# Attention in fp32 with clustered masks, then two mixing layers, on one core: TensorE's order pinned by unit

## The chip, the cores and the metric

The kernel runs on one core of a Trainium2 chip. The metric is the device time of one execution in microseconds (us); the median of three runs before the change is 664.98 us (664.54 to 666.16).

## What is computed

`reference` runs three stages on fp32 data, with 2 batches, 8 heads, 768 positions and a head size of 64 (so a model width of 512):

```python
mask = q_assign[:, :, :, None] == k_assign[:, :, None, :]        # 16 clusters per head
scores = np.where(mask, scale * q @ k.T, -1e9)
attn = np.exp(scores - scores.max(-1)) ; attn /= attn.sum(-1) + 1e-9
x = (attn @ v)                       # put back to (2, 768, 512)
u = x + token_mlp(x) ; x = u + relu(u @ w_ch1) @ w_ch2
x = x + w_tok_r @ (x cos(x @ w_theta)) + w_tok_i @ (x sin(x @ w_theta))
out = x + relu(x @ w_ch)
```

The change lies in the first of these stages, the attention.

## The kernel before, in words

The attention takes up roughly the first 240 us of the span. It is cut into 48 **units**: for each of 16 (batch, head) pairs, three blocks of 256 query positions. One unit passes through three functions:

- `scores` (L380): two score tiles, one per 128 queries. A tile is 4 products of 128x384 (L397 and L398: the high part of q with k, then the low part of q together with the mask's rows). It lands in a PSUM buffer of the pool `ps_s`, which has **two** buffers, so a tile needs the buffer of the tile two before it. VectorE (DVE) takes the maximum (L400, `nm`), ScalarE (ACT) the exponential (L402, `e`), and after the exponential the buffer is free.
- `turn` (L409): 12 transposes of 128x128 on TensorE (PE) of the unit's two `e` tiles, four to each of three PSUM tiles `t` (L417). The pool `ps_t` has **three** buffers. ACT copies the first two out, DVE the third (L420, L422, `p`).
- `values` (L426): the product of `p` with v. The program issues six matrix products, the profile shows twelve records of 128x256 in column halves of 64 (L438, `o`), into the **one** buffer of the pool `ps_o`. ACT copies one half out (L445, `tmp`), DVE adds the other to it (L447, `xt`).

The loop over `n` (L485) calls `scores` of unit n, `turn` of unit n-1 and `values` of unit n-2. Other work of the loop also uses `ps_t`: once in six units the masks of the next pair of heads (L246 `sim`, one tile; L270 `pp`, one tile, read by DVE at L271 `oh`), and once in six units `natural` (L451), which transposes a finished pair of heads (L460 `x`, two tiles of 4 and 2 transposes) and multiplies each block by its reciprocal sum on DVE (L462 `xn`, six instructions). The `x` tiles come up eight times in all: at six places with a `pp` beside them, a seventh near the end of the loop and the last behind it. Near the end, the weights of the next stage are also prepared inside the loop (L109 to L116 on ACT, DVE and POOL).

The order in which an engine's instructions stand is set by a scheduler when the program is built (`schedule_with_timeline_sim=True`, L799 of the launch); each engine then runs its own list from top to bottom. `tc.issue_after(i)` forces the instructions of its block that are on i's engine behind i; it adds no wait between engines. Before the change, only `values` was tied in this way (the call at L532 and L533, behind the last transpose that the text had issued). Scores and transposes were free to be placed by the scheduler.

Of the kernel before, what the change touches and what calls it, by code (L numbers as in the profile page):

```python
# [49 lines left out]
def tile_model(ctx: ExitStack, tc: tile.TileContext, qT, kT, v, cent, w1, w2, wc1, wc2, wth, wri, wch, out):  # L50


    nc = tc.nc
# [14 lines left out]
    marks = {}  # L68
# [92 lines left out]
    with ExitStack() as actx:  # L161
# [12 lines left out]
        def warm_up(n):  # L174
            for _ in range(n):
                nc.tensor.matmul(wps[:, :256], warm[:, :P], warm, start=True, stop=True)
# [203 lines left out]
        def scores(b, h, u, ops):  # L380

            qh, ql, k1, kk, _ = ops
            es = []
            for j in range(2):
                qt = 2 * u + j
                c = slice(qt * P, qt * P + P)
                ps = ps_s.tile([P, 2, 512], F32, tag="s", name=f"s{b}{h}{qt}")
                first = (b, h, u) == (0, 0, 0)
                if first:

                    for half in range(2):
                        nc.tensor.matmul(ps[:, half, :NH], qh[:, c], k1[:, half * NH : half * NH + NH], start=True, stop=False)
                with tc.issue_after(marks["cl"].ins) if first else nullcontext():
                    for half in range(2):
                        n = slice(half * NH, half * NH + NH)
                        if not first:
                            nc.tensor.matmul(ps[:, half, :NH], qh[:, c], k1[:, n], start=True, stop=False)  # L397
                        marks["scores"] = nc.tensor.matmul(ps[:, half, :NH], ql[:, c], kk[:, n], start=False, stop=True)  # L398
                nm = small.tile([P, 1], F32, tag="nm", bufs=4, name=f"nm{b}{h}{qt}")
                marks["max"] = nc.vector.tensor_reduce(out=nm, in_=ps[:, :, :NH], axis=AX.XY, op=ALU.max, negate=True)  # L400
                e = ap.tile([P, S], F32, tag="e", bufs=4, name=f"e{b}{h}{qt}")
                marks["exp"] = nc.scalar.activation(  # L402
                    out=e.rearrange("p (a n) -> p a n", a=2), in_=ps[:, :, :NH], func=AF.Exp,
                    bias=nm, accum_out=sums[b, h // 2][:, qt, h % 2 : h % 2 + 1],
                )
                es.append(e)
            return es

        def turn(b, h, u, es):  # L409

            pr = []
            for j in range(NT // 2):
                ps = ps_t.tile([P, 2, 256], F32, tag="t", name=f"t{b}{h}{u}{j}")
                for i in range(2):
                    for a in range(2):
                        kt = 2 * j + a
                        marks["turn"] = nc.tensor.transpose(ps[:, a, i * P : i * P + P], es[i][:, kt * P : kt * P + P], ident)  # L417
                p = ap.tile([P, 2, 256], F32, tag="p", bufs=PB, name=f"p{b}{h}{u}{j}")
                if KINDS[j] == "A":
                    marks["pA"] = nc.scalar.activation(out=p, in_=ps, func=AF.Copy)  # L420
                else:
                    marks["pV"] = nc.vector.tensor_copy(out=p, in_=ps)  # L422
                pr.append(p)
            return pr

        def values(us):  # L426


            if us[-1][0] == len(units) - 1:
                ps = ps_s.tile([P, 2, 512], F32, tag="s", name="olast")[:, 0, :]  # L430
            else:
                ps = ps_o.tile([P, 512], F32, tag="o", name=f"o{us[0][0]}")
            outs = []
            for i, (n, pr, vs) in enumerate(us):
                po = ps[:, 256 * i : 256 * i + 256]
                for kt in range(NT):
                    r = 64 * (kt % 2)
                    nc.tensor.matmul(  # L438
                        po[r : r + 64, :], vs[:, kt, :], pr[kt // 2][:, kt % 2, :], start=kt < 2, stop=kt >= NT - 2,
                        tile_position=(0, r),  # L440
                    )
                outs.append((units[n], po))
            for (b, h, u), po in outs:
                tmp = ap.tile([64, 256], F32, tag="tmp", bufs=2, name=f"tmp{b}{h}{u}")
                marks["tmp"] = nc.scalar.activation(out=tmp, in_=po[64:128, :], func=AF.Copy)  # L445
                r0 = 64 * (h % 2)
                nc.vector.tensor_tensor(  # L447
                    out=xts[b, h // 2][r0 : r0 + 64, u * 256 : u * 256 + 256], in0=po[0:64, :], in1=tmp, op=ALU.add
                )
# [25 lines left out]
        with tc.issue_after(marks["cst"].ins):  # L475
            ops = {heads[0]: prep_pair_first(raws) + (vs00,)}
# [5 lines left out]
        units = [(b, h, u) for b, h in heads for u in range(NT // 2)]  # L482
        es, prs = {}, {}
        late, group = [], []
        for n in range(len(units) + SKEW):  # L485
            if n < len(units):
                b, h, u = units[n]
                if u == 0 and h % 2 == 0:
                    sums[b, h // 2] = small.tile([P, NT, 2], F32, tag="sm", bufs=2, name=f"sm{b}{h}")
                    xts[b, h // 2] = ap.tile([P, S], F32, tag="xt", bufs=2, name=f"xt{b}{h}")  # L490
                if n != 1:
                    es[n] = scores(b, h, u, ops[b, h])
                if n == 0:
                    next(first, None)
                    place(1, ms[0, 0])
                    scored = marks["scores"]
                    es[1] = scores(*units[1], ops[b, h])
                    with tc.issue_after(marks["max"].ins):
                        ops[heads[1]] = prep_first(*heads[1])
                    marks["scores"] = scored  # L500
                    for w, k in zip(WARM[1:], ("cps", "sim", "scores")):
                        with tc.issue_after(marks[k].ins):
                            warm_up(w)
                h1 = n // 3 + 1
                if 1 < h1 < len(heads) and u == PREP[h1 % 2]:
                    b2, h2 = heads[h1]
                    ops[b2, h2] = prep(b2, h2, ms[b2, h2 // 2])
                p1 = n // 6 + 1
                if p1 < len(heads) // 2:
                    pr = heads[2 * p1][0], heads[2 * p1][1] // 2  # L510
                    if n % 6 == PAIR_AT[0]:
                        raws = load_pair(*pr)
                    if n % 6 == PAIR_AT[1]:
                        split_pair(*pr, raws)
                    if n % 6 == PAIR_AT[2]:
                        gen = masks(*pr)
            if n >= 3:
                for _ in range(PACE):
                    next(gen, None)
            if n == 42:  # L520
                mctx.close()
            if 0 <= n - 1 < len(units):
                prs[n - 1] = turn(*units[n - 1], es.pop(n - 1))
            if n < 3:
                with tc.issue_after((marks["turn"] if n else marks["scores"]).ins):
                    for _ in range(PACE):
                        next(gen, None)
            if 0 <= n - SKEW:
                b, h, u = units[n - SKEW]
                group.append((n - SKEW, prs.pop(n - SKEW), ops[b, h][4]))  # L530
                if len(group) == GROUP:
                    with tc.issue_after(marks["turn"].ins):  # L532
                        values(group)  # L533
                    group = []
                if h % 2 == 1 and u == NT // 2 - 1:
                    late.append((n + 1, b, h // 2))
            while late and (n >= late[0][0] or n == len(units) + SKEW - 1):
                _, b, pr = late.pop(0)
                natural(b, pr)
            if n in X_AT:  # L540
                tok_x(0, X_AT.index(n), part, "pp")
            if n in W1_AT:
                with tc.issue_after(marks["exp"].ins):
                    i = len(w1s)
                    w1s.append(load_w(w1[:, i * 512 : i * 512 + 512], f"w1_{i}", W1_AT[n]))
            if n == len(units):
                with tc.issue_after(marks["tmp"].ins), tc.issue_after(marks["pA"].ins), tc.issue_after(marks["pV"].ins):
                    for i in range(NT // 2):
                        w2s.append(load_w(w2[:, :, i * 256 : i * 256 + 256], f"w2_{i}", "pv"))
# [197 lines left out]
    for n in range(len(steps) + 2):  # L747
        if n < len(steps):
            t, b = steps[n]
# [53 lines left out]
```

## Time and profile before

| What | Value |
|---|---|
| median of 3 runs | 664.98 us |
| the profiled execution | 664.99 us, its span 663.3 us |
| PE busy | 646.8 us (98%), 3591 matmuls |
| DVE / ACT / POOL busy | 401.2 / 344.9 / 257.6 us |
| costliest groups of the attention on PE | L417 80.5 us, L397 71.9 us, L438 71.2 us, L398 65.3 us (they overlap) |

The page's busy share of PE counts matmuls that overlap in the array's pipeline, so 98% does not say that nothing can be won. The chain of waits is of more use: it lists, in order of time, the work that led to the last instruction, with the time by which each piece moved the end forward. Where a piece of the chain is not PE's, PE stood and waited for it. One unit's pieces there add up to the unit's time.

### The profile page before, as it was taken

The page shows a single profiled execution, that of the slowest core. Times are in us where ns is not written, and L with a number is a line of the kernel's source. Part 1 is how long each engine was busy: PE and PEld are TensorE (multiplying, and loading weights), DVE is VectorE, ACT ScalarE, POOL GpSimd, SP SyncE. Part 2 cuts the span into 40 slices and gives each one's busy share as a digit, 9 for nine tenths or more (in the row PEclk, how much of TensorE's full clock was granted, in tenths as well). Part 3 has the DMA queues.
Part 4 walks back from the last instruction along what each step waited for, and adds up shares of the span by engine and source line. Part 5 has one row for each costly group of instructions (what it writes and reads, how often), then busy time and mean ns, then how long its engine had stood idle before and what let it go on. Part 6 is the DMA issues. An engine that isn't in the chain of part 4 may idle for free.

```text
span 663.3 us, 9795 instructions
## 1 busy us (share of the span) xinstructions
PE 646.8 (98%) x3591; PEld 517.7 (78%) x3591; DVE 401.2 (60%) x649; ACT 344.9 (52%) x653; POOL 257.6 (39%) x231
## 2 busy tenths in 40 slices
PE   7999999999999989999999999999999999999998
PEld 4777777777777758878888888888887878888886
DVE  5877778687787776466665442546677694531212
ACT  5676776777767863256444320428487673320000
POOL 6230312364031131138887520603467796541000
PEclk9999999999999998999999999999999999999999
DMA  8554755444555121023433310310021424300001
GB/s 294 160 138 105 169 123 144 120 117 114 113 123 124 37 96 47 18 67 124 154 133 127 126 53 14 95 33 0 1 85 42 128 88 127 114 20 33 16 33 47
DMA packets 24207, 61.42 MB, mean 93 GB/s; under 512 B 4256, under 2 KB 7520, under 8 KB 24160
## 3 DMA queue, kind: packets, MB, share of 16 engines
q1 hardware_dynamic: 24160, 60.80, 32.3%
q8 instruction: 28, 0.46, 0.3%
q14 instruction: 19, 0.16, 0.1%
HBM read 39.65 MB, written 3.15 MB: 65 GB/s over the span
## 4 chain that ended last, share of the span: by engine, by line
PE 86%; ACT 4%; DVE 3%; POOL 3%; issue 2%; DMA 2%; SPq 0%; POOLq 0%; ACTq 0%
PE o L438 10%; PE t L417 9%; PE s L397 5%; PE r L126 5%; PE r L127 5%; PE r L128 5%; PE c L126 5%; PE c L127 5%; PE c L128 5%; PE s L398 5%; PE y L128 4%; PE y L127 4%; PE y L126 4%; PE po L126 2%; PE po L128 2%
## 5 line engine op out<-in xcount | busy, mean ns | idle before, releaser
L402 ACT ACTIVATE e<-s,nm 128x768 f32<-128x768 f32 x96 | 86.7, 905 | 29.4 <-DVE nm L400 28.1
L400 DVE TENSOR_REDUCE nm<-s 128x1 f32<-128x768 f32 x96 | 90.5, 951 | 18.9 <-PE s L398 18.0
L417 PE MATMUL t<-ident,e 128*128 128x128 f32 x576 | 80.5, 275 | 0.6 <-ACT p L420 0.5
L417 PEld LDWEIGHTS t<-ident,e 128*128 128x128 f32 x576 | 66.4, 140 | 16.0 <-issue 9.4
L397 PE MATMUL s<-k,qh 128*128 128x384 f32 x188 | 71.9, 382 | 2.5 <-ACT e L402 2.3
L438 PE MATMUL o<-p,vs 128*64 128x256 f32 x564 | 71.2, 388 | 0.0
L398 PE MATMUL s<-k,q 128*128 128x384 f32 x192 | 65.3, 343 | 2.4 <-DVE q L279 2.4
L420 ACT ACTIVATE p<-t 128x512 f32<-128x512 f32 x96 | 52.2, 594 | 25.4 <-PE t L417 25.0
L126 PE MATMUL r<-ul,c_h 128*128 128x512 f32 x144 | 56.5, 396 | 0.4 <-DVE ul L90 0.4
L126 PE MATMUL y<-zl,k_h 128*128 128x512 f32 x144 | 56.1, 390 | 0.0
L128 PE MATMUL y<-zh,k_h 128*128 128x512 f32 x144 | 56.1, 390 | 0.0
L127 PE MATMUL r<-uh,c_l 128*128 128x512 f32 x144 | 56.1, 390 | 0.0
L127 PE MATMUL y<-zh,k_l 128*128 128x512 f32 x144 | 56.0, 389 | 0.0
L127 PE MATMUL c<-c_h,rl 128*128 128x512 f32 x144 | 56.0, 390 | 0.0
L128 PE MATMUL r<-uh,c_h 128*128 128x512 f32 x144 | 56.0, 390 | 0.0
L128 PE MATMUL c<-c_h,rh 128*128 128x512 f32 x144 | 55.9, 390 | 0.0
L126 PE MATMUL c<-c_l,rh 128*128 128x512 f32 x144 | 55.2, 391 | 0.0
L438 PEld LDWEIGHTS o<-p,vs 128*64 128x64 f32 x564 | 36.3, 136 | 22.7 <-issue 5.9
L116 POOL TENSOR_TENSOR c_f<-c_f,c_raw 128x512 uint32<-128x512 uint32 x24 | 31.6, 1318 | 44.7 <-issue 31.3
L80 POOL TENSOR_SCALAR qh<-ql 128x768 fp32r<-128x768 f32 x7 | 5.8, 835 | 100.9 <-DMA qh<-qh 100.8
L397 PEld LDWEIGHTS s<-k,qh 128*128 128x128 f32 x188 | 35.4, 188 | 11.1 <-ACT e L402 5.6
L398 PEld LDWEIGHTS s<-k,q 128*128 128x128 f32 x192 | 36.7, 192 | 3.8 <-ACT k L276 3.4
(192 smaller groups left out, 1387.9 us busy)
## 6 DMA issues: line engine op xcount, KB each, us to landing
c_raw<-wc SPq DMA_DIRECT2D x24, 512.0 KB, 3.3
k_raw<-wri SPq DMA_DIRECT2D x18, 512.0 KB, 3.5
qh<-qh SPq DMA_DIRECT2D x28, 192.0 KB, 3.0
k<-kh SPq DMA_DIRECT2D x28, 192.0 KB, 3.8
ql<-qT SPq DMA_DIRECT2D x8, 384.0 KB, 3.2
kl<-kT SPq DMA_DIRECT2D x8, 384.0 KB, 4.6
vs<-v SPq DMA_DIRECT2D x16, 192.0 KB, 2.4
w_raw<-w SPq DMA_DIRECT2D x6, 512.0 KB, 4.1
```

Of the source, the lines that this page charges most:

```text
L80: nc.gpsimd.tensor_scalar(out=h, in0=x, scalar1=1.0, scalar2=0.0, op0=ALU.mult, op1=ALU.add)
L116: nc.gpsimd.tensor_tensor(out=wu, in0=wu, in1=lo, op=ALU.add)
L126: nc.tensor.matmul(ps, ah, bl, start=first and i == 0, stop=False)
L127: nc.tensor.matmul(ps, al, bh, start=False, stop=False)
L128: nc.tensor.matmul(ps, ah, bh, start=False, stop=last and i == n - 1)
L397: nc.tensor.matmul(ps[:, half, :NH], qh[:, c], k1[:, n], start=True, stop=False)
L398: marks["scores"] = nc.tensor.matmul(ps[:, half, :NH], ql[:, c], kk[:, n], start=False, stop=True)
L400: marks["max"] = nc.vector.tensor_reduce(out=nm, in_=ps[:, :, :NH], axis=AX.XY, op=ALU.max, negate=True)
L402: marks["exp"] = nc.scalar.activation(out=e.rearrange("p (a n) -> p a n", a=2), in_=ps[:, :, :NH], func=AF.Exp, bias=nm, accum_out=sums[b, ...
L417: marks["turn"] = nc.tensor.transpose(ps[:, a, i * P : i * P + P], es[i][:, kt * P : kt * P + P], ident)
L420: marks["pA"] = nc.scalar.activation(out=p, in_=ps, func=AF.Copy)
L438: nc.tensor.matmul(po[r : r + 64, :], vs[:, kt, :], pr[kt // 2][:, kt % 2, :], start=kt < 2, stop=kt >= NT - 2, tile_position=(0, r),)
```

## The change

Two ties are added. `scores` of unit n goes behind the last product of `values` that the text has issued (unit n-3), and `turn` of unit n-1 goes behind the last score product that the text has issued (unit n). With the tie that was there, the list on PE becomes: scores of n, transposes of n-1, values of n-2, scores of n+1, and so on. No arithmetic, buffer or transfer is changed. `marks` is a dictionary of the last instruction of each kind.

```diff
-                    nc.tensor.matmul(
+                    marks["o"] = nc.tensor.matmul(
                         po[r : r + 64, :], vs[:, kt, :], pr[kt // 2][:, kt % 2, :], start=kt < 2, stop=kt >= NT - 2,
                         tile_position=(0, r),
                     )
...
                 if n != 1:
-                    es[n] = scores(b, h, u, ops[b, h])
+                    with tc.issue_after(marks["o"].ins) if "o" in marks else nullcontext():
+                        es[n] = scores(b, h, u, ops[b, h])
...
             if 0 <= n - 1 < len(units):
-                prs[n - 1] = turn(*units[n - 1], es.pop(n - 1))
+                with tc.issue_after(marks["scores"].ins) if n > 2 else nullcontext():
+                    prs[n - 1] = turn(*units[n - 1], es.pop(n - 1))
```

In the built program PE's list changes in the attention alone. DVE's and ACT's lists change there too, since the scheduler places their work anew around it. The lists of POOL and of SP, which issues the DMAs, stay as they were.

A plain unit on PE (in the names `s_435` is a score tile, `t_467` a tile of transposes, `e_387` and `e_396` the two exponentials that it is made from):

```order
 L398 MATMUL s_435<-k_1_152,q_1_150 128x384
-L417 MATMUL t_467<-ident,e_387 128x128 x2
-L417 MATMUL t_474<-ident,e_387 128x128 x2
-L417 MATMUL t_481<-ident,e_387 128x128 x2
 L397 MATMUL s_444<-k_243,qh_242 128x384
 L398 MATMUL s_444<-k_1_152,q_1_150 128x384
 L397 MATMUL s_444<-k_243,qh_242 128x384
 L398 MATMUL s_444<-k_1_152,q_1_150 128x384
+L417 MATMUL t_467<-ident,e_387 128x128 x2
 L417 MATMUL t_467<-ident,e_396 128x128 x2
+L417 MATMUL t_474<-ident,e_387 128x128 x2
 L417 MATMUL t_474<-ident,e_396 128x128 x2
```

The transposes of the first exponential stood between the two score tiles; now both score tiles come first and the twelve transposes follow in one piece.

The same engine at a place where `natural` stands. Ahead of these rows both programs have one score tile (`s_1126`), the six `x` transposes and `pp`:

```order
 L397 MATMUL s_1135<-k_941,qh_940 128x384
 L398 MATMUL s_1135<-k_1_152,q_1_150 128x384
-L397 MATMUL s_1181<-k_941,qh_940 128x384
-L398 MATMUL s_1181<-k_1_152,q_1_150 128x384
-L397 MATMUL s_1181<-k_941,qh_940 128x384
-L398 MATMUL s_1181<-k_1_152,q_1_150 128x384
 L417 MATMUL t_1150<-ident,e_1063 128x128 x2
 L417 MATMUL t_1150<-ident,e_1072 128x128 x2
```

The first score tile of the next unit (`s_1181`) stood between this unit's scores and the transposes. Now the transposes follow at once, and that tile comes behind the values.

DVE at the same place, in the changed program:

```order
L400 TENSOR_REDUCE nm_1131<-s_1126 128x1
L447 TENSOR_TENSOR xt_921<-o_1099,tmp_1106 64x256
L462 TENSOR_TENSOR xn_66<-x_1112,ri_1109 128x128
L462 TENSOR_TENSOR xn_67<-x_1112,ri_1109 128x128
L462 TENSOR_TENSOR xn_68<-x_1112,ri_1109 128x128
L462 TENSOR_TENSOR xn_69<-x_1112,ri_1109 128x128
L462 TENSOR_TENSOR xn_70<-x_1121,ri_1109 128x128
L462 TENSOR_TENSOR xn_71<-x_1121,ri_1109 128x128
L271 SCALAR_TENSOR_TENSOR oh_1144<-pp_1145,eqT_1076 128x384
L400 TENSOR_REDUCE nm_1140<-s_1135 128x1
```

Here `xt` has moved: it stood behind `oh` and now stands ahead of the six `xn`, which are what empties the two `x` tiles.

## Rows read from the trace of the kernel before

**Rows 1.** The page: busy time by engine, and the chain's shares by engine.
```profile
PE 646.8 (98%) x3591; PEld 517.7 (78%) x3591; DVE 401.2 (60%) x649; ACT 344.9 (52%) x653; POOL 257.6 (39%) x231
...
PE 86%; ACT 4%; DVE 3%; POOL 3%; issue 2%; DMA 2%; SPq 0%; POOLq 0%; ACTq 0%
```

**Rows 2.** Busy time by stretch: stretch, length, engines; then the granted clock, DMA.
```profile
160.00:180.00 20.00, 19.38 (x143) 15.18 (x141) 15.50 (x29) 13.99 (x30) 0.00 (x0) 1.00 0.39 92
...
248.00:250.00 2.00, 1.48 (x4) 1.25 (x5) 1.50 (x3) 0.63 (x1) 0.23 (x1) 0.72 0.01 4
```

**Rows 3.** Chain, a plain unit from 29.14 us: start, length, engine, tile, line.
```profile
30.59 0.37 PE s L397
...
31.48 0.66 PE t L417 x6
...
33.49 1.45 PE o L438 x12
```

**Rows 4.** Chain, 66 to 78 us: after values, and around the masks' products.
```profile
68.72 0.81 PE t L417 x6
...
73.03 0.78 PE sim L246 x8
73.81 0.59 PE t L417 x4
```

**Rows 5.** Chain, 100 to 120 us: a place with x tiles where PE waits.
```profile
109.49 0.37 PE s L397
...
110.42 0.97 DVE nm L400
...
111.47 1.00 ACT e L402 x2
...
112.52 0.44 PE s L397
...
113.48 1.31 PE t L417 x12
114.80 1.45 PE o L438 x12
```

**Rows 6.** Waits of PE, 50 to 200 us: total, times, longest.
```profile
PE s L397 <- ACT e L402: 1.9, 3, 0.6
```

**Rows 7.** Timeline of DVE, 110 to 114 us.
```profile
111.30 0.40 DVE L447 TENSOR_TENSOR xt<-o,tmp 64x256 f32<-64x256 f32 x1
111.63 1.26 DVE L462 TENSOR_TENSOR xn<-x,ri 128x128 f32<-128x128 f32 x6
112.82 0.54 DVE L271 SCALAR_TENSOR_TENSOR oh<-pp,eqT 128x384 f32<-128x384 f32 x1
```

**Rows 8.** Chain, 76 to 94 us: a place with x tiles without a wait.
```profile
82.45 0.81 PE x L460 x6
83.26 0.16 PE pp L270
...
84.81 1.31 PE t L417 x12
```

**Rows 9.** Timeline of ACT, 204 to 223 us: how close its instructions follow.
```profile
205.75 1.08 ACT L420 ACTIVATE p<-t 128x512 f32<-128x512 f32 x2
206.72 0.91 ACT L402 ACTIVATE e<-s,nm 128x768 f32<-128x768 f32 x1
...
207.59 0.67 ACT L109 ACTIVATE w_f<-w_raw 128x512 f32<-128x512 f32 x1
```

**Rows 10.** Chain, values' products at three units far apart.
```profile
58.64 1.45 PE o L438 x12
...
198.44 1.45 PE o L438 x12
...
237.84 1.51 PE o L438 x12
```

**Rows 11.** Chain and waits near the end of the attention, 196 to 250 us.
```profile
208.30 0.44 DVE w_raw L112
...
234.93 0.44 PE t L417 x2
...
PE g L126 <- DVE gl L148: 2.6, 1, 2.6
PE s L397 <- ACT e L402: 0.5, 1, 0.5
```

## The prediction

> **What bounds the kernel now.** I read the page first: PE is busy 98% of the span and holds 86% of the chain [rows 1]. So time can come only from PE's own pieces or from the gaps between them. The change touches the attention alone (PE's later list is unchanged), so I went to the stretches of the attention: 19.38 of 20 us busy at a granted clock of 1.00, which is 2.4 GHz [rows 2]. Then I read the chain unit by unit. From the end of one unit's values to the end of the next, a plain unit is 0.90 for a score tile (its first product 0.37, the other three 0.18 each), 0.66 for six transposes, 0.70 for the second tile, 0.66 again, and 1.45 for the values [rows 3]. That is **4.35 us, all of it PE's**. Where the chain leaves PE, something is late: this happens at every second place with x tiles, where a score tile waits for the exponential that empties its buffer [rows 5]. Between 50 and 200 us these are the only waits of PE, three of 0.6 us [rows 6].
>
> **The change part by part.**
>
> *The plain unit.* The same products, in another order. One thing has a price: the first product after values is dearer. Scores cost 0.37 there instead of 0.18 [rows 3], so 0.19 more; six transposes cost 0.81 [rows 4] instead of 0.66 [rows 3], so 0.15 more; the masks' products cost 0.78 and the transposes behind them 0.59 [rows 4] where four cost 0.44 (two thirds of 0.66), 0.15 more again. So each return to full-width products costs something, once per unit, and nothing else in the order does. After the change scores follow the values nearly always: 4.35 us. Before, 21 of the 48 values are followed by transposes; those units are 0.04 shorter. 21 x 0.04 = 0.8 us is what the new order costs here. The Trainium skill, TensorEngine Tiling (Array Packing), section Key Properties, says that changing the tiling mode drains TensorE, and makes no difference by what comes next. By that rule the 0.8 us would be nothing, and the sum below +2.9 instead of +3.7; the rows show 0.19 and 0.15, and they decide.
>
> *The wait that goes.* At the place of [rows 5], from 109.49 to 114.80 are 5.31 us. The work in it is 0.91 for the first tile, 0.66 for six x transposes, 0.16 for pp [rows 8], twice 0.71 for the second tile and the next unit's first, and 1.31 for the transposes: 4.46. So the wait costs 0.85 us, with the refill behind it (the first score product takes 0.44 instead of 0.18). It is paid three times. In the changed order that score tile comes after the values, 2.8 us later, and its buffer is long free.
>
> *The wait that comes.* The transposes now stand right behind the scores, and their three PSUM buffers are those that the two x tiles and pp have just filled. The first must wait for the fourth xn of DVE. DVE's list there is maximum, xt, six xn, oh, as the order shows; the trace has this very sequence once in two places [rows 5, 7]. The maximum starts 110.42 and xt 111.30, xn at 111.63; six take 1.26, so they start 0.20 apart and the fourth ends about 112.50. PE could begin the transposes at 109.49 + 0.91 + 0.66 + 0.16 + 0.71 = 111.93. It begins at 112.54 and pays the refill (two transposes took 0.44 after a wait [rows 11], 0.22 is their share of six in [rows 3]): **0.83 us lost**. In the list before, the next unit's score tile (0.71) stood in this gap; with it the transposes find the buffers empty [rows 8]. And it now happens at every such place, not at every second: six times. The second and third transposes' buffers (last xn 112.89, oh 113.36) are free when PE comes to them. The maximum of the second tile waits behind oh on DVE, and ACT's exponential behind that; both have until the next unit.
>
> *A cycle of six units.* Changed: four plain units 17.40, one with the masks' products 4.35 + 0.78 = 5.13, one with x tiles 4.35 + 0.66 + 0.16 + 0.83 = 6.00; together 28.53. Before: from 58.64 to 198.44 are 139.80 us for five cycles [rows 10], 27.96 each; at both ends the same score tile is ahead. Five cycles: 142.65 - 139.80 = **+2.8 us**. This holds the first three points, for these thirty units.
>
> *The first units.* Up to 58.64 one masks' unit has one dear return less (-0.15), and the first place trades 0.85 for 0.83: **-0.2 us**.
>
> *The last ten units.* Weight preparation lies between DVE's and ACT's attention work. DVE's xt of one unit now stands behind both maxima and a weight step of 0.44 [rows 11], and values need the single buffer that xt empties: maxima from 0.93 after the values' end, 0.88 + 0.36 + 0.88 + 0.40 for the four steps, so 3.5 against 2.9 at which PE arrives. I take 0.7 with the refill. A like wait meets the seventh place of x tiles, where a buffer hangs on a copy on ACT behind an exponential: 0.7. The wait of 0.5 for an exponential goes [rows 11]. With some dear returns: **+1.1 us**, between 0 (if the weight steps find the gaps that they find now) and 2.5 (four such waits).
>
> *What is behind.* The next stage starts with a wait of 2.6 us on weights and on the same DVE steps [rows 11]; its start hangs on the last tmp, so it shifts with the attention. The clock there is 0.72, partly at 1.2 GHz [rows 2], in either case. No DMA moves. I take the shift as carried to the end.
>
> Sum: 2.8 - 0.2 + 1.1 = +3.7 us. The profiled execution took 664.99, the median is 664.98, so both give **668.7 us**, 0.6% slower.
>
> **The rivals.**
>
> *DVE is in time* (not slower). If the fourth xn came 0.6 us earlier, or PE refilled without loss, the six waits of 0.83 (5.0 us) vanish and the waits of [rows 5] go for good: 668.7 - 5.0 = 663.7. For it: at the places of [rows 8] the xn start right behind x and nothing waits. Against it: there a unit's first maximum is done before x; in the changed list it starts only when the tile ends, and xt is put in between, as at 111.30 [rows 7]. It decides at 0.6 us of DVE.
>
> *ACT becomes the bound* (slower still). In most changed units ACT's list is exponential, two copies, exponential. From the values' end: tile 0.91, maximum 0.97, 0.09 to start, exponential 0.87 to the next instruction, copies 0.97 (205.75 to 206.72), second exponential 1.00 [rows 5, 9]: 4.81. With 0.04 + 0.44 PE could end its next second tile's first product at 5.29; it gets there at 4.35 + 0.91 + 0.18 = 5.44. The slack is 0.15 us per unit. If real spacing eats it and 0.1 more, thirty units cost 3 us: 671.7; with 0.2, 674.7. The rows speak for slack, barely.
>
> *The pins change nothing that costs.* The order rows exclude that nothing moves; gain and loss could still cancel to 665.
>
> **How the numbers follow.** A measurement can tell about 0.3% from no change, 2.0 us here. Forecast 0.72, its own range 667 to 671 (the last units' bounds, x waits of 0.7 to 0.9); DVE in time 0.13; ACT the bound 0.12; cancelling 0.03. Slower: 0.72 + 0.12, less 0.04 for the forecast's low edge, 0.80. Faster by over 2.0 us needs the first rival and no loss at the end: 0.04. Same: 0.16. The range leaves out most of the first rival and the upper half of the second: 665.8 to 672.5.
>
> **What would show it.** In the profile after: PE waiting for DVE's xn ahead of transposes (L417) six times, about 0.6 us idle each, and no longer for exponentials at L397 between 50 and 200 us; plain units of 4.35, x units of 6.0, masks' units of 5.1; values waiting once or twice near 210 us. If PE waits at L397 in plain units, ACT was the bound. If x units take 5.2, the DVE reading was wrong. If the attention ends 3.7 us later and the whole does not, a later wait took it up.

## The result, and the profile after

The changed kernel takes 671.45 us (median of four runs, 670.4 to 672.25) against 665.57 for the kernel before in the same measurement: a ratio of 1.0085, 95% interval 1.0062 to 1.0107. It is **slower by 0.85%**, 5.9 us. The forecast was 668.7, slower by 3.7, with a range to 672.5. Sign and mechanism hold; the forecast loss is too small. Two places account for that: the attention itself, which loses 4.5 us instead of 3.7, and a later stage that the forecast took as rigid.

The profiled execution took 671.89 us. Its page, busy time by engine and the chain's shares, against [rows 1]:

```profile
PE 647.9 (97%) x3591; PEld 520.8 (78%) x3591; DVE 404.4 (60%) x649; ACT 341.4 (51%) x653; POOL 258.3 (39%) x231
...
PE 35%; POOL 3%; issue 2%; DMA 2%; ACT 2%; DVE 0%; POOLq 0%; ACTq 0%; DVEq 0%
```

PE is busy about as long as before (647.9 against 646.8 us) in a span longer by 6.8: most of what was added is idle time, not work. The chain now gives PE only 35% and has no row of the attention: followed back from the end, it leaves PE near 392 us for the weight preparation. This is the second place; it is taken up below.

The waits of PE from 50 to 200 us, against [rows 6]:

```profile
PE t L417 <- DVE xn L462: 3.7, 5, 0.7
```

And from 200 to 260 us, against the last rows of [rows 11]:

```profile
PE g L126 <- DVE gl L148: 2.6, 1, 2.6
PE x L460 <- ACT p L420: 0.9, 1, 0.9
PE t L417 <- DVE xn L462: 0.7, 1, 0.7
PE t L417 <- ACT p L420: 0.7, 1, 0.7
PE o L438 <- DVE xt L447: 0.7, 1, 0.7
```

Scores no longer wait for an exponential (L397 has no row), and six times the transposes wait for xn: five at 50 to 200 us, the sixth just behind. One such place in PE's timeline (start, length, instruction, in brackets the idle time ahead and what ended it):

```profile
109.51 1.52 PE L438 MATMUL o<-p,vs 128*64 128x256 f32 x12
110.95 0.45 PE L397 MATMUL s<-k,qh 128*128 128x384 f32 x1
...
111.76 0.82 PE L460 MATMUL x<-ident,xt 128*128 128x128 f32 x6
112.42 0.33 PE L270 MATMUL pp<-eqT,ltri 128*128 128x384 bf16 x1
112.44 0.47 PE L397 MATMUL s<-k,qh 128*128 128x384 f32 x1
...
114.18 1.50 PE L417 MATMUL t<-ident,e 128*128 128x128 f32 x12 [0.74 <-DVE xn L462]
115.61 0.44 PE L438 MATMUL o<-p,vs 128*64 128x256 f32 x2
```

And DVE's timeline there:

```profile
111.96 0.96 DVE L400 TENSOR_REDUCE nm<-s 128x1 f32<-128x768 f32 x1 [1.36 <-PE s L398]
112.83 0.41 DVE L447 TENSOR_TENSOR xt<-o,tmp 64x256 f32<-64x256 f32 x1
113.17 1.26 DVE L462 TENSOR_TENSOR xn<-x,ri 128x128 f32<-128x128 f32 x6
114.35 0.54 DVE L271 SCALAR_TENSOR_TENSOR oh<-pp,eqT 128x384 f32<-128x384 f32 x1
```

DVE stands idle for 1.36 us, then takes maximum, xt and six xn one after the other. PE starts the last product of its second score tile at 113.10; these products follow 0.17 us apart, so the transposes could start at about 113.27. They start at 114.18, when by the prediction's reckoning (six xn, about 0.2 us apart) the fourth xn is out. From values to values this unit takes 115.61 - 109.51 = 6.10 us.

In the same timeline, values of three units far apart (before: 58.57, 198.37 and 237.81) and the first product behind the attention:

```profile
58.34 1.52 PE L438 MATMUL o<-p,vs 128*64 128x256 f32 x12
...
201.50 1.51 PE L438 MATMUL o<-p,vs 128*64 128x256 f32 x12
...
243.00 1.52 PE L438 MATMUL o<-p,vs 128*64 128x256 f32 x12
...
245.07 0.49 PE L126 MATMUL g<-xl,w_h 128*128 128x512 f32 x1
```

Five cycles of six units: 143.16 us (before 139.80). From the first values to `g`, the length called **the attention** from here on: 245.07 - 24.73 = 220.34 us, before 239.88 - 24.05 = 215.83. So the attention loses 4.5 us; the rest of the difference between the two profiles lies ahead of it (0.7) and behind it (1.6).

### The profile page after: what moved, and what is told of

It reads as the page before. It is cut to its first block, busy times and chain, and to the rows that moved or that the text cites. A ratio compares the mean times of both kernels' runs of the same rounds, so it can differ in the third digit from the quotient of the medians.

```text
span 670.1 us, 9839 instructions
## 1 busy us (share of the span) xinstructions
PE 647.9 (97%) x3591; PEld 520.8 (78%) x3591; DVE 404.4 (60%) x649; ACT 341.4 (51%) x653; POOL 258.3 (39%) x231
## 5 line engine op out<-in xcount | busy, mean ns | idle before, releaser
L417 PE MATMUL t<-ident,e 128*128 128x128 f32 x576 | 72.5, 274 | 5.6 <-DVE xn L462 4.4
L397 PE MATMUL s<-k,qh 128*128 128x384 f32 x188 | 69.6, 370 | 0.0
L397 PEld LDWEIGHTS s<-k,qh 128*128 128x128 f32 x188 | 35.5, 189 | 19.0 <-ACT e L402 9.0
```

## The experiments

The table gives for each kernel the start of the first values, the attention's length, the time from `g` to the end of the span (all from the profiled execution) and the median of the timed runs. The kernel before ran beside each group: 664.87 us with the first four, 665.31 with the next four, 665.46 with the last two.

| Kernel | first values | attention | behind it | median | ratio to before, interval |
|---|---|---|---|---|---|
| before | 24.05 | 215.83 | 423.4 | | |
| changed | 24.73 | 220.34 | 425.0 | 671.45 | 1.0085, 1.0062 to 1.0107 |
| e1_turn_only | 23.54 | 214.95 | 425.3 | 667.37 | 1.0033, 1.0014 to 1.0052 |
| e2_scores_only | 23.38 | 219.79 | 424.7 | 670.13 | 1.0087, 1.0061 to 1.0114 |
| e3_x_first | 24.30 | 216.91 | 424.8 | 667.33 | 1.0033, 1.0017 to 1.0048 |
| e4_after_again | 24.55 | 220.28 | 428.4 | 671.05 | 1.0099, 1.0073 to 1.0126 |
| e5_before_again | 23.50 | 215.78 | 425.8 | 667.2 | 1.0020, 0.9999 to 1.0041 |
| e6_before_th_tied | 25.26 | 215.83 | 422.6 | 664.27 | 0.9985, 0.9969 to 1.0002 |
| e7_after_th_tied | 25.28 | 220.36 | 421.4 | 668.65 | 1.0043, 1.0028 to 1.0059 |
| e8_turn_th_tied | 25.29 | 214.64 | 423.4 | 664.55 | 0.9982, 0.9968 to 0.9996 |
| e9_x_oh_first | 23.60 | 214.12 | 423.1 | 662.54 | 0.9958, 0.9942 to 0.9973 |
| e10_free_tail | 24.42 | 212.51 | 422.6 | 661.21 | 0.9940, 0.9923 to 0.9957 |

The attention's length repeats within 0.1 us between executions of one order (220.34, 220.28 and 220.36; 215.83, 215.78 and 215.83). The other two columns don't: they move by some us between executions of the same code.

Part of that is the granted clock of TensorE, which is 1.00 at 2.4 GHz and 0.50 at 1.2 GHz. Stretch from 240 to 260 us, busy time of the engines, then the granted clock, in e6_before_th_tied and e7_after_th_tied:

```profile
240.00:260.00 20.00, 17.44 (x81) 13.09 (x78) 14.12 (x26) 9.94 (x18) 5.72 (x6) 0.91 0.24 79
240.00:260.00 20.00, 16.91 (x97) 12.21 (x98) 14.98 (x30) 11.25 (x22) 7.03 (x7) 1.00 0.33 106
```

Neither has the wait behind the attention that is described below. The one whose clock stays at 1.00 takes 421.4 us behind the attention, the other 422.6. The time of a whole execution goes with its mean granted clock too: the kernel before has a median of 663.6 us in the 8 executions at 1.000, 665.2 in the 34 at 0.995 and 667.0 in the 14 at 0.992 (the executions beside the three groups). At 0.995 the changed kernel has 670.3 (5 executions), 5.1 more. The clock is not free of the waits, though: in e4_after_again it is 0.83 between 390 and 400 us, right behind a wait of PE of 2.2 us, and 1.00 there in the first profile of the changed kernel, whose longest wait at that place is 0.8.

### Which tie brings the loss

e1_turn_only undoes the tie of the scores, e2_scores_only that of the transposes:

```diff
-                    with tc.issue_after(marks["o"].ins) if "o" in marks else nullcontext():
-                        es[n] = scores(b, h, u, ops[b, h])
+                    es[n] = scores(b, h, u, ops[b, h])
```

> Only the tie of the transposes is kept; scores are free, as before the change. The built order then puts the next unit's score tile behind the x transposes at five of the six x places, the two x tiles stand around the values, and only the first place keeps the old wait for the exponential. Theory (the loss is the six waits of the transposes for DVE's xn, which the tie of the scores brings): a cycle of six units is 4 x 4.35 + 5.13 + (4.35 + 0.66 + 0.16) = 27.70 us, five cycles 138.5 against 139.80 before and 143.16 in the changed kernel; PE waits for xn ahead of transposes nowhere between 60 and 200 us; the whole is 663.5 to 665 us, 0.1 to 0.3% below the kernel before. Rival 1 (each tie takes scheduling freedom and costs its part): about 668.5 us. Rival 2 (the wait for xn comes with the transposes' tie): waits of 0.6 us at the x places and 670 to 671.5 us.

```diff
-                with tc.issue_after(marks["scores"].ins) if n > 2 else nullcontext():
-                    prs[n - 1] = turn(*units[n - 1], es.pop(n - 1))
+                prs[n - 1] = turn(*units[n - 1], es.pop(n - 1))
```

> Only the tie of the scores is kept; transposes are free. The built order has the second score tile behind the x transposes and the transposes behind it, as in the changed kernel, at all six places; the masks' first products stand where they cost one more dear return. Theory (the scores' tie brings the loss): x units of 6.0 to 6.1 us, six waits for xn of 0.6 to 0.7 us, masks' units up to 0.15 longer than 5.13; 670 to 672 us in all, like the changed kernel. Rival 1 (each tie costs its part): about 668.5. Rival 2 (the transposes' tie brings it): 665 to 666.

Waits of PE from 50 to 200 us, e1_turn_only:

```profile
PE s L397 <- ACT e L402: 2.6, 5, 0.7
```

The same view of e2_scores_only:

```profile
PE t L417 <- DVE xn L462: 3.7, 5, 0.7
```

With the scores' tie alone the waits for xn are all there, the x units take 6.11 us, the masks' units 5.30, and the time is that of the changed kernel. With the transposes' tie alone none of them is there. So the scores' tie brings them. In e1_turn_only the expectation failed in two points. I had expected a wait for the exponential at the first x place alone; but it comes at four of the other five places too, because one score tile stands ahead of values there and the next right behind them. Five cycles take 198.60 - 57.82 = 140.78 us, not 138.5; the attention still gains 0.9 over before, by its last ten units (37.8 us against 39.4). And the whole is 0.33% slower than before, though its attention is shorter, so the reason lies outside the attention.

### Taking the wait away

e3_x_first keeps both ties, and ties the scores behind the x transposes:

```diff
-                    nc.tensor.transpose(ps[:, i, :], xt[:, (q0 + i) * P : (q0 + i + 1) * P], ident)
+                    marks["o"] = nc.tensor.transpose(ps[:, i, :], xt[:, (q0 + i) * P : (q0 + i + 1) * P], ident)
```

> Both ties are kept, and the x transposes are pulled ahead of the next unit's scores (the scores are tied behind them): values, x, pp, score tile, score tile, transposes. Theory (the x units lose 0.83 us because xn starts behind a maximum and meets the transposes at once): with two score tiles (1.4 us) between x and the transposes, xn (1.26 us) is done in time; no wait for xn; what may remain is the third transpose tile waiting for oh, up to 0.45 us. x units of 5.2 to 5.6 instead of 6.1, six times: 3 to 5 us below the changed kernel, 666.5 to 669 us. Rival (the six us come from dear returns, the end of the attention or the stages behind, not from these waits): within 1 us of the changed kernel, 670.5 to 672.

The built order at an x place is values, x, score tile, pp, score tile, transposes (pp behind the first tile, not ahead of it as expected). The x units take 5.60 us, the attention is 3.4 us shorter than the changed kernel's (216.91), the time is 667.33, 3.7 below e4_after_again, which ran beside it: within what was expected, and the rival is out. What is left of a wait, in PE's timeline at the second x place of e3_x_first:

```profile
81.38 0.88 PE L460 MATMUL x<-ident,xt 128*128 128x128 f32 x6
...
83.66 1.03 PE L417 MATMUL t<-ident,e 128*128 128x128 f32 x8
84.94 0.66 PE L417 MATMUL t<-ident,e 128*128 128x128 f32 x4 [0.25 <-ACT p L420]
```

DVE's timeline there:

```profile
82.07 1.08 DVE L462 TENSOR_TENSOR xn<-x,ri 128x128 f32<-128x128 f32 x5 [0.93 <-PE x L460]
...
83.60 0.94 DVE L400 TENSOR_REDUCE nm<-s 128x1 f32<-128x768 f32 x1
84.47 0.53 DVE L271 SCALAR_TENSOR_TENSOR oh<-pp,eqT 128x384 f32<-128x384 f32 x1
84.93 0.93 DVE L400 TENSOR_REDUCE nm<-s 128x1 f32<-128x768 f32 x1
```

xn now starts as soon as the x tiles are there. The row of PE names an ACT copy, but PE goes on at 84.94, just as oh gives way to the next maximum on DVE (84.93). The third transpose tile needs the buffer of pp, and oh, which empties it, stands behind a maximum. The kernel e9_x_oh_first, below, tests that reading.

### What repeats, and the wait behind the attention

e4_after_again and e5_before_again are the two kernels without any edit.

> The changed kernel once more, unaltered, to part what repeats from what is chance. In its first profile 0.7 us came ahead of the first values (at 1.2 GHz for longer in the first 20 us) and 1.6 us behind the attention, with a new wait of PE for DVE's rl near 392 us. Theory 1 (both belong to the change, since the later lists meet the shifted weight steps at another moment): values of the first unit start at 24.7 again, the wait for rl of 0.8 is there again, span about 670. Theory 2 (both are run to run): values of the first unit start near 24.05, the span is 668 to 669, and the wait for rl is gone or elsewhere. Time 670.5 to 672 by the first, 669 by the second.

> The kernel before once more, unaltered. In four profiles of altered kernels PE waits near its stage c (for ACT's rh 0.3 to 2.2 us, for DVE's rl 0.8), behind a weight step of th on ACT that waits for its DMA; the first profile of before has no such wait. Theory 1 (the changed attention shifts the weight pipeline, so the wait belongs to the change): ratio 1.000, and no wait of PE for rh or rl over 0.3 us between 360 and 400 us. Theory 2 (the DMAs land later in some executions, whatever the kernel): waits for rh or rl of 0.5 us or more here too.

Waits of PE from 360 to 400 us, where the first profile of before has none; e4_after_again:

```profile
PE c L126 <- ACT rh L645: 2.2, 1, 2.2
PE c L127 <- DVE rl L646: 0.8, 1, 0.8
```

The same view of e5_before_again:

```profile
PE c L127 <- DVE rl L644: 0.8, 1, 0.8
PE c L126 <- ACT rh L643: 0.2, 1, 0.2
```

The wait comes in the kernel before too; what it costs varies: nothing and 1.0 us in two profiles of before, 1.4 (0.8 and 0.6) and 3.0 in two of the changed kernel. So neither theory holds alone: there is such a wait whatever the kernel, and whether the changed one has more of it on average stays open. The 0.7 us ahead of the first values are chance: PE's work is the same up to there in all kernels, and the kernel before itself has 24.05 and 23.50, with a granted clock of 0.83 and 1.00 between 10 and 20 us; both profiles of the changed kernel have 0.66 there, but with the tie of th (below) before and changed have 25.26 and 25.28, at 0.70 both. One more thing: identical code came out 0.20% apart here, so differences below about 0.3% mean nothing in this table. That too goes with the clock: at a mean granted clock of 0.995, e5_before_again has 665.3 us (5 of its 12 executions) against the 665.2 of the kernel before, and the other 7 have a lower clock.

How the wait comes about, in ACT's timeline of the changed kernel:

```profile
384.50 1.07 ACT L645 ACTIVATE rh<-r 128x512 fp32r<-128x512 f32 x2
389.07 0.67 ACT L110 ACTIVATE th_raw<-th_raw 128x512 uint32<-128x512 uint32 x1 [3.50 <-DMA th_raw<-wth]
389.65 0.64 ACT L109 ACTIVATE th_f<-th_raw 128x512 f32<-128x512 f32 x1
390.19 1.06 ACT L645 ACTIVATE rh<-r 128x512 fp32r<-128x512 f32 x2
```

ACT stands for 3.5 us before a weight step of th, whose DMA has not landed, and two rh that PE needs next stand behind it in ACT's list. In e4_after_again the same row has 5.43 us of idle time. That idle time is not the cost by itself: ACT's list behind the attention is the same in the kernel before, and there the same step stands 3.59 us while PE waits for nothing:

```profile
382.10 0.65 ACT L110 ACTIVATE th_raw<-th_raw 128x512 uint32<-128x512 uint32 x1 [3.59 <-DMA th_raw<-wth]
```

What differs is when the step comes, counted from the start of `g`: 142.2 us before, 144.0 and 145.7 in the two profiles of the changed kernel, with waits at c of 0, 1.4 and 3.0 us. The chain of the changed kernel shows the same from the other side:

```profile
385.07 3.92 DMA th_raw<-wth
...
390.85 0.69 DVE th_f L113
391.54 0.61 DVE rl L646
...
392.20 0.50 PE c L127
```

Yet the first product of th comes at 441 us in the kernel before, 50 us and more after these steps. e6_before_th_tied and e7_after_th_tied put the steps of its four weights behind the last rh of the block ahead, in the kernel before and in the changed one; e8_turn_th_tied does it in e1_turn_only:

```diff
+    rh = marks["rh"]
...
-            wt = [load_w(wth[:, c * 512 : c * 512 + 512], f"th_{c}") for c in range(NC)]
+            with tc.issue_after(rh.ins):
+                wt = [load_w(wth[:, c * 512 : c * 512 + 512], f"th_{c}") for c in range(NC)]
```

(`marks["rh"]` is set at the ACT instruction of `up`.)

> The kernel before with one tie in the stages behind the attention: the four th weights' steps on ACT stand behind the last rh of the block ahead, so no rh stands behind a wait for a th DMA. PE's order is unchanged. If before loses nothing there (its first profile shows no wait): 664.5 to 665.2 us, as without the tie. If it loses in the typical execution what the altered kernels lose: 663 us. If the delayed th weights come too late for their first use 55 us later: slower, 666 or more.

> The changed kernel with the same tie of the th weights. From the first values to the first product behind the attention the changed kernel takes 220.3 us in both profiles, before 215.8: 4.5 us. Theory (what it loses beyond these 4.5 is the wait at c behind th on ACT): the waits for rh and rl are gone, 669 to 669.7 us, 1.5 to 2 below the changed kernel and 4.5 above the tied before. Rival (a later wait takes the gain up, or the loss is elsewhere): 671 us as without the tie.

> Only the transposes' tie in the attention, with the tie of the th weights. The attention of the first experiment took 214.95 us against 215.83 before, 0.9 less, and yet that kernel was 2.5 us slower in the median. Theory (what it lost was the wait at c): 663.5 to 664.5 us, at or below the kernel before and 3 below the first experiment. Rival (the loss lies elsewhere, for instance in the first 20 us, at 1.2 GHz for longer in some executions): 666.5 to 667.5.

ACT's timeline of e7_after_th_tied, where three th steps now come without idle time:

```profile
387.64 0.58 ACT L645 ACTIVATE rh<-r 128x512 fp32r<-128x512 f32 x1
388.12 0.67 ACT L109 ACTIVATE th_f<-th_raw 128x512 f32<-128x512 f32 x1
388.68 1.81 ACT L110 ACTIVATE th_raw<-th_raw 128x512 uint32<-128x512 uint32 x3
```

The fourth weight's step still stands 4.62 us for its DMA (to 395.65), but the next rh on ACT comes only at 422 us. In all three kernels PE has no wait from 360 to 400 us, and no other takes its place up to 470 in e6 and e7. The changed kernel gains 2.4 us against e4_after_again (671.05 to 668.65, 0.35 below the expected range), the kernel before 1.0 (its interval just holds no change; 664.27 lies between the two cases of its expectation), e1_turn_only 2.8 (664.55, 0.05 above the expected range). With the tie in both, changed less before is 668.65 - 664.27 = **4.4 us**, which agrees with the 4.5 of the attention carried to the end. It does not prove that nothing else is left: the two intervals together leave about 1.5 us either way, and the executions at a mean granted clock of 0.994 and 0.995 alone give 668.8 - 664.0 = 4.9. e8_turn_th_tied, 664.55, stands at e6_before_th_tied's 664.27: the 1.2 us that its attention gains don't show in the time.

### A version that beats both

e9_x_oh_first is e7_after_th_tied with the x transposes ahead as in e3_x_first, and with the step of the masks that holds pp and oh ahead of the scores at these units, whose maxima are tied behind oh. e10_free_tail ties the scores only up to unit 39.

```diff
+        def oh_first(n):
+            return n > 6 and n % 6 == 3 and n < 42
+
+        def nc_oh(n):
+            return tc.issue_after(marks["oh"].ins) if oh_first(n) else nullcontext()
...
+                if oh_first(n):
+                    for _ in range(PACE):
+                        next(gen, None)
...
-                    with tc.issue_after(marks["o"].ins) if "o" in marks else nullcontext():
+                    with tc.issue_after(marks["o"].ins) if "o" in marks and n < 40 else nullcontext(), (
+                        nc_oh(n)
+                    ):
                         es[n] = scores(b, h, u, ops[b, h])
...
-            if n >= 3:
+            if n >= 3 and not oh_first(n):
```

(`oh_first(n)` holds for n = 9, 15, ..., 39, the units at the six x places; the `n < 40` is e10_free_tail's alone, e9_x_oh_first ties the scores to the end.)

> The changed kernel with the tie of the th weights, the x transposes ahead of the next scores as in the third experiment, and at these places the masks' product pp and its reader oh ahead of the scores' maxima (a tie on DVE). Theory (the 0.43 us that the x units of the third experiment still cost is the third transpose tile waiting for the buffer that oh reads, with oh behind a maximum): x units of 4.35 + 0.66 + 0.16 = 5.17 us and no wait of PE in them; the attention 6 x 0.43 = 2.6 us shorter than the third experiment's 216.9, 214.3; the whole 668.65 - (220.36 - 214.3) = 662.6 us. Rival (ACT's second exponential then comes late, because both maxima move back by oh): a wait of scores for e, and 664 or more.

> As the kernel e9_x_oh_first, but the scores are tied only up to unit 39, so that the last ten units are placed by the scheduler as in the first experiment, where 198.60 to 236.41 took 37.8 us against 41.5 in the changed kernel and 39.4 before. Theory (pinning the scores costs about 2 us in these units, where weight steps lie between DVE's and ACT's attention work): 1 to 2 us below e9_x_oh_first, 661 us, and below both kernels. Rival (at the change from tied to free a score tile stands ahead of values and waits for an exponential): 1 us of it is lost there, 662.5.

DVE's timeline at the second x place of e9_x_oh_first:

```profile
80.93 1.08 DVE L462 TENSOR_TENSOR xn<-x,ri 128x128 f32<-128x128 f32 x5 [0.84 <-PE x L460]
...
82.45 0.54 DVE L271 SCALAR_TENSOR_TENSOR oh<-pp,eqT 128x384 f32<-128x384 f32 x1
82.92 1.80 DVE L400 TENSOR_REDUCE nm<-s 128x1 f32<-128x768 f32 x2
```

The chain of e9_x_oh_first at the first x place:

```profile
51.21 1.45 PE o L438 x12
52.65 0.81 PE x L460 x6
...
54.16 0.18 PE pp L270
...
55.03 1.31 PE t L417 x12
```

The x units take 5.13 us, no wait of PE is left between 50 and 200 us, and the time is 662.54 (expected 662.6). So the last 0.43 us was oh behind the maximum, not the ACT copy that the profile had named: PE's order at this place is the same in e3_x_first and here, and here PE takes all twelve transposes in one piece from 82.51, 1.47 us long, though the ACT copies start only at 83.15. With the last units free the attention falls to 212.51, and one wait remains from 50 to 240 us, the score tile at the change from tied to free that the rival had named. View of waits, e10_free_tail:

```profile
PE s L397 <- ACT e L402: 0.7, 1, 0.7
```

It takes 661.21 us, ratio 0.9940 (0.9923 to 0.9957): 0.6% below the kernel before and 1.5% below the changed one. Of the 0.6%, the tie of th alone is worth 0.15% by e6_before_th_tied, which is not clear of noise.

## Why the prediction was right, and where its size was off

- **The plain unit**: 4.35 forecast, 4.34 to 4.37 measured. Units whose values are followed by transposes took 4.30 to 4.33 before, those followed by scores 4.35 to 4.36: the 0.04 that I charged is there, within 0.02. The Trainium skill (TensorEngine Tiling (Array Packing), section Key Properties) says that a change of the tiling mode drains TensorE, and nothing on what comes next. Read as one price whatever comes next, as I read it in the prediction, it would leave no such difference; these rows don't bear that reading out, by 0.02 to 0.06 us a unit.
- **The wait that goes**: right, no L397 row between 50 and 200 us.
- **The wait that comes**: right in place, number and cause (six, for xn, behind maximum and xt); the size was 0.83 and is 6.10 - 4.35 - 0.82 = 0.93 (0.82 is the work of the x transposes and pp). PE goes on 1.01 us after the first xn starts (113.17 to 114.18), where I had worked out 0.91. Six times 0.1.
- **The cycle**: 28.53 forecast, 143.16 / 5 = 28.63 measured; +3.4 us instead of +2.8 over five.
- **The first units**: -0.2 forecast. Up to the values at 58.34 the changed kernel is 0.9 us shorter (33.61 against 34.52 from the first values), but there the next unit's score tile (0.71) is not yet done, which before it is: -0.2.
- **The last ten units**: +1.1 forecast. From 201.50 to 243.00 are 41.50 us, before 198.37 to 237.81 are 39.44; less the same tile 41.50 - 39.44 - 0.71 = +1.35. Values wait for xt (0.7) and x for a copy (0.9) as forecast; a third wait, transposes for a copy (0.7), I had not seen.
- **Sum for the attention**: 3.7 forecast; 3.36 - 0.20 + 1.35 = 4.5 by these parts, which is the difference of the profiles. The two terms that were too small are the six waits (by 0.6 in all) and the last ten units (by 0.25).
- **What is behind**: this is the step that failed. "I take the shift as carried to the end" fits the attention's 4.5 us (4.4 with th tied in both kernels); but what follows is not rigid. The stage c has a wait of its own, from none to 3 us, that hangs on when a DMA of th lands, and the granted clock moves the same time. "No DMA moves" holds for the list of the DMAs, not for when they land: the step of th that waits for one comes 142.2 us behind the start of `g` before, 144.0 and 145.7 in the changed kernel. I had read one profile of before, which shows no such wait. In the profiles, 1.4 of the 1.6 us that the changed kernel loses behind the attention is this wait. Of the timed 5.9 us, about 0.8 goes with the clock (5.1 is left at a mean granted clock of 0.995; part of that may come from the wait itself), and the interval of that first measurement, 4.1 to 7.1 us, does not part 5.9 from 4.5. So how much of the rest is the change's and how much chance stays open, since the kernel before has the same wait in some executions. That the measured 671.45 lies inside the stated range is in part luck: it is above the forecast's own 671, in the part that was kept for the rival of ACT, which did not come.
- **The rivals**: DVE was not in time (e9_x_oh_first, where by a changed order nothing waits at the x places, shows what that is worth: x units of 5.13 instead of 6.10, six times, 5.8 us against the 5.0 that I had reckoned). ACT did not become the bound: no L397 wait, and plain units of 4.35. Gain and loss did not cancel.

## What to carry to other kernels

A tie on one engine decides what stands between a producer and the instruction that needs its buffer back: ask for each tie which filler work it forbids, and whether the engine that empties the buffer starts before or behind other work there. When a wait is found, look at the list of the engine that ends it; moving one short step ahead of a long one (oh ahead of a maximum) took another 2.8 us off the attention (216.91 to 214.12), after the 3.4 of the better order on TensorE. A stage that shows no wait in one profile may still hang by a thread on a DMA: an instruction that waits for a load should not stand ahead of one that the busiest engine needs, above all if what it loads is needed only 50 us later. And where two kernels differ by under 1%, compare executions at the same mean granted clock: here the time of the unaltered kernel went by 3 us with it.

## What the runs showed of the hardware that was not expected

- The idle time of the same ACT instruction before a th load was 3.50 us in one execution of the changed kernel and 5.43 in another, with the same lists on every engine; the wait of PE for rh behind it took 0.6 and 2.2 us. In the kernel before 3.59 us of it cost PE nothing.
- Between 10 and 20 us the granted clock of TensorE lay between 0.66 and 1.00 for the same work, and the first values started between 23.38 and 25.29 us. At 1.00 they started at 23.38 to 23.60, at 0.83 at 23.54 and 24.05, at 0.66 at 24.30 to 24.73, and latest at 0.70, at 25.26 to 25.29; so the clock of that stretch is not all of it.
- Identical code, timed as if it were a changed kernel, came out at 1.0020 (0.9999 to 1.0041).
- The mean granted clock of an execution went from 0.989 to 1.000 for the same program, and the kernel before took a median of 667.0 us at 0.992 and 663.6 at 1.000.
- The releaser that a row names can be one that was long done: 84.94 in e3_x_first names ACT, and moving a DVE instruction took the wait away.
